# Splitting the last output tile of a fused attention and feed-forward kernel, with an older start order

## The chip, the cores and the metric

One NeuronCore of a Trainium2 chip. The metric is the device time of one execution in microseconds, as a median over runs; a profiled execution beside it says where the time goes. The engines that matter: TensorE (PE, with its weight loads shown apart as PEld), VectorE (DVE), ScalarE (ACT), GpSimd (POOL), and SyncE (SP), which issues most transfers. Each runs its own list of instructions in order and waits on semaphores.

## The reference

Linear attention for 8 batches, 8 heads, 576 positions and head size 64, then a feed-forward layer with a swish that has one beta for each of its 2048 units:

```python
q_s = softmax(q, over the head's 64 numbers)
k_s = softmax(k, over the 576 positions)
kv  = einsum('bhsd,bhse->bhde', k_s, v)
x   = einsum('bhsd,bhde->bhse', q_s, kv)      # to 4608 x 512
h   = x @ w_in                                # 4608 x 2048
g   = h * sigmoid(beta * h)
out = g @ w_out                               # 4608 x 512, float32
```

Inputs and output are float32; inside, the kernel multiplies in bfloat16 and sums in float32.

## The kernel before

The 4608 tokens go through in nine slabs of 512: slab t < 8 holds the first 512 positions of batch t, and slab 8 the last 64 positions of all eight batches. For each slab there is a first product (16 units f of 128 hidden columns, each 4 matmuls over the input pairs m, into a PSUM bank, then ACT's Silu into `GT`) and a second product (four token tiles u of 128, each 16 matmuls over f with 512 output columns, then a copy to `O2S` and a store). "Input pair" m is a pair of heads, 128 of the 512 inputs. Attention work for the next batch is woven into these matmuls by tick counts: `todo` holds (tick, step), and `tick()` runs what is due.

Everything is in the program order of one Python list; `Program` derives the waits from keys read and written and sends each instruction to its engine's list. So a line's place in the program sets its place in its engine's order, transfers on SP's and ACT's lists too.

The start, batch 0 and batch 1, is written out by hand:

- Loads on SP: q and k of batch 0, v of batch 0 (`load_v`, four transfers), then W_in in blocks (`load_win(c, m)`: c is a group of 512 hidden columns, that is 4 units; m the input pair), then W_out (`load_wout`), with batch 1's q, k, v between. W_in and W_out land as float32 in stage buffers; `cast_win` casts W_in blocks to bf16 on POOL or DVE, and `scale_wout` multiplies W_out tile f by 1/beta on DVE (L555).
- Batch 0: exponentials on ACT, the normalising of q on DVE and POOL, transposes of q on PE (`t_steps`, with a copy `QT<-PS`, L384), K-V products (`kv_mm`), `ksum_inv` and `kvd` (KVD is the K-V product divided by the sums, L518 and L403), the output product `out_now` with its copy `XT<-PS` (L530).
- `by_m` runs four units of the first product at once, input pair by input pair, so that a weight block is used as soon as it is cast; `pass1_tile` runs one unit over all its four pairs. `FIRST` says how many units go by `by_m`: 16 of slab 0 and 5 of slab 1.
- In slab 0's second product all four token tiles go side by side, f outermost, so that each W_out tile is used when it has been scaled. At ticks 107 and 112 the transposes of batch 1's q come in, at 115 and 117 the K-V products of its first two head pairs, at 122 and 123 `out_now` for them.

W_in's and W_out's hidden columns are ordered so that a row of a weight transfer is contiguous: units 0 to 7 are interleaved in pairs (`f // n * n`, `f % n` with n = 2), units 8 to 15 in fours.

From the second batch on the transposes are done by the transfer engines, and the attention steps are spread over the slabs' ticks.

Slab 8's output tile u is copied by DVE (L713) when its 16 matmuls are done and stored by `store8` in two transfers of 64 rows, one issued by SP and one by ACT.

Of the kernel before, what the change touches and what calls it, by code (L numbers as in the profile page):

```python
# [156 lines left out]
def bass_efficient_attn_shen__then__act_swish_beta_kernel(  # L157
# [12 lines left out]
    with ExitStack() as es:  # L170
# [367 lines left out]

        STAGE = (WST[0], WST[1], O2S[1], O2S[0])
# [3 lines left out]
        def load_wout(f, n=4):  # L543
            c, x = f // 4, f % 4
            if f < 8:
                a = bass.AP(wout_h, 512 * c * DM, [[2 * DM, 128], [256 * DM, 2], [1, 2 * DM]])
                o = bass.AP(STAGE[c], 0, [[4 * DM, 128], [2 * DM, 2], [1, 2 * DM]])
            else:
                a = bass.AP(wout_h, (512 * c + x) * DM, [[4 * DM, 128], [1, n * DM]])
                o = bass.AP(STAGE[c], x * DM, [[4 * DM, 128], [1, n * DM]])  # L550
            add(SP, lambda e: e.dma_start(o, a), w=SKEY[c][x:x + n], slot=f"wst{f}")  # L551
# [19 lines left out]
        def turn_beta():  # L571
            for g, n, o in ((4, 4, 0), (2, 2, 0), (2, 2, 256)):
                for k_ in range(n):
                    mm(bass.AP(PS[KB], 16 + o // 128 + k_, [[512, 128], [4, g]]),
                       bass.AP(BT, o + k_, [[512, g], [n, 128]]), IDF[0:g, 0:g],
                       True, True, r=["bt", "idf"], w=[("ps", KB)], bk=KB, tr=True)
# [33 lines left out]
        load_v(0, 4, (0, 1, 2))  # L610
        load_win(0, 0, 1)
        load_v(0, 4, (3,))
        for c in range(4):
            for m in range(0 if c else 1, NM, 1 if c < 2 else 2):
                load_win(c, m, 1 if c < 2 else 2)
# [3 lines left out]
        cast_win(0, 0, POOL)  # L619
        cast_v(0, 3)  # L620
        cast_win(0, 2, POOL)
        cast_win(0, 3, POOL)
        cast_win(1, 0, POOL)
# [9 lines left out]
        kvd(0, 1, 1, 0)  # L633

        orot = [0]

        def pass1_mm(t, f, m, bk):
            x = XT8 if t == 8 else XT[t % 2]
            rd = [("xt8", p_) for p_ in range(4)] if t == 8 else [("xt", t % 2, m)]
            n = 2 if f < 8 else 4  # L640
            l = bass.AP(WIN, m * DFF + 128 * (f // n * n) + f % n, [[NM * DFF, 128], [n, 128]])
# [24 lines left out]
        FIRST = (16, 5)  # L666
# [4 lines left out]
        cast_win(0, 1, DVE)  # L671
        out_now(0, 1, 6, ACTE)
        at = by_m(0, 0, 4)
        at(0, 0, 3)
        kv_mm(0, 3, 1, 0, D + 1)
        at(0, 3)
        out_now(0, 2, 0, ACTE)
        ksum_inv(0, 1, 3, 1, D, 1)
        kvd(0, 3, 1, 0)
        at(1)  # L680
        out_now(0, 3, 7, DVE)
# [5 lines left out]
        for c in range(1, 4):  # L687
            for m in range(1 if c == 1 else 0, NM):
# [3 lines left out]
        for g in (4, 8, 12):  # L692
# [3 lines left out]
        for e_ in range(2):  # L696
            homes_ek(1, e_, [("win", 3, NM - 1)])
# [24 lines left out]
        def store8(u):  # L722
# [174 lines left out]
```

## Time and profile before

| what | value |
|---|---|
| median of 4 runs | 286.53 us (286.35 to 286.71) |
| the profiled execution's own time | 286.16 us |
| its span, first to last instruction | 284.4 us |
| PE busy | 275.3 us, 97% of the span |
| ACT / DVE / POOL busy | 177.9 / 117.2 / 39.5 us |
| matmuls of 512 columns, first product / second product | 131.4 us / 131.4 us |
| first matmul with weights of W_in | 13.51 us |
| first matmul of the second product | 28.61 us |
| first output product of batch 1 | 43.41 us |
| last copy of an output tile | 280.55 us, 0.69 us long |
| granted TensorE clock | 1.0 |

Times in the lists are microseconds from the span's start. A line of the timeline gives start, duration, engine, source line, operation, tiles written and read, shapes, how many such instructions are merged, and in brackets how long the engine was idle before and which instruction ended that. Group lines give busy time in us and the mean of one instruction in ns.

### The profile page before, as it was taken

Reading aid. Unit: us, or ns where it says so; the run is one execution under the profiler, and the core shown is the slowest. Engines: PE = TensorE matmul, PEld = TensorE weight load, DVE = VectorE, ACT = ScalarE, POOL = GpSimd, SP = SyncE. Lnnn points to the kernel's source line nnn. Section 1 sums busy time; section 2 is a strip of 40 time slices with the busy share of each in tenths; the row PEclk is TensorE's granted clock in tenths of the full one; section 3 lists DMA queues with packets and bytes.
Section 4 is the critical chain, followed back from the end, with each engine's and each line's share of the span. In section 5 each row is a group of like instructions: output and inputs, shape, how many; then the busy total and the mean of one; then the engine's idle time right before and its main releaser. Section 6 shows DMA issues by size and latency. Waiting matters only on the chain.

```text
span 284.4 us, 3851 instructions
## 1 busy us (share of the span) xinstructions
PE 275.3 (97%) x1543; PEld 135.1 (48%) x1573; DVE 117.2 (41%) x216; ACT 177.9 (63%) x242; POOL 39.5 (14%) x59
## 2 busy tenths in 40 slices
PE   6899999999999999999999999999999999999994
PEld 2545454445455445544554445444544444444441
DVE  4863896019881348123831473045705200110021
ACT  5967777989978926795579637892650185028400
POOL 6622041307122033100230000000000000000000
PEclk9999999999999999999999999999999999999999
DMA  7999999996998999217970033003500120021022
GB/s 245 349 393 400 388 386 377 352 385 121 312 362 228 369 362 298 39 38 262 364 95 1 2 149 72 2 1 129 111 2 0 45 105 0 0 92 58 0 74 74
DMA packets 41306, 50.07 MB, mean 176 GB/s; under 512 B 20292, under 2 KB 28484, under 8 KB 40136
## 3 DMA queue, kind: packets, MB, share of 16 engines
q1 hardware_dynamic: 40416, 48.77, 53.5%
q10 hardware_dynamic: 872, 1.06, 1.0%
q8 instruction: 12, 0.20, 0.3%
q14 instruction: 6, 0.05, 0.1%
HBM read 36.71 MB, written 9.44 MB: 162 GB/s over the span
## 4 chain that ended last, share of the span: by engine, by line
PE 83%; DMA 7%; SPq 5%; ACT 2%; issue 1%; DVE 1%; ACTq 0%
PE PS L366 83%; DMA O2S<-in_moe_w_in_dram 4%; DMA KF<-in_k_dram 3%; SPq L259 2%; SPq L249 2%; SPq L562 1%; ACT EK L317 1%; ACT QT L384 0%; DVE WIN L566 0%; DVE O2S L713 0%; ACT GT L645 0%; ACT XT L530 0%; ACT O2S L713 0%; SPq L551 0%; ACTq L140 0%
## 5 line engine op out<-in xcount | busy, mean ns | idle before, releaser
L645 ACT ACTIVATE GT<-PS,BETA 128x512 bf16<-128x512 f32 x144 | 96.5, 688 | 79.2 <-PE PS L366 79.1
L366 PE MATMUL PS<-WOUT,GT 128*128 128x512 bf16 x563 | 131.4, 379 | 1.3 <-ACT QT L384 0.6
L366 PE MATMUL PS<-XT,WIN 128*128 128x512 bf16 x561 | 131.4, 379 | 0.6
L366 PEld LDWEIGHTS PS<-XT,WIN 128*128 128x128 bf16 x576 | 60.1, 106 | 59.5 <-POOL WIN L566 0.9
L366 PEld LDWEIGHTS PS<-WOUT,GT 128*128 128x128 bf16 x576 | 54.2, 98 | 63.5 <-DVE WOUT L555 0.9
L713 DVE COPY O2S<-PS 128x512 f32<-128x512 f32 x34 | 23.4, 687 | 110.5 <-PE PS L366 110.5
L366 PE MATMUL PS<-VB,EK 128*128 128x65 bf16 (+2 forms) x306 | 35.8, 191 | 1.1 <-ACT VB L351 0.6
L351 POOL CAST VB<-VF 128x576 bf16<-128x576 f32 x31 | 23.1, 747 | 73.8 <-DMA VF<-in_v_dram 36.2
L307 ACT ACTIVATE EK<-KF 64x1152 bf16<-64x1152 f32 x24 | 27.8, 1157 | 0.4
L366 PEld LDWEIGHTS PS<-VB,EK 128*128 128x128 bf16 x306 | 22.0, 98 | 7.7 <-ACT VB L351 0.5
L332 DVE TENSOR_REDUCE QS<-EQ 128x8 f32<-128x512 bf16 (+1 forms) x22 | 20.1, 914 | 3.7 <-ACT EQ L295 3.5
L441 DVE CAST XT<-PS 128x512 bf16<-128x512 f32 x24 | 16.4, 690 | 10.9 <-PE PS L366 10.9
L295 ACT ACTIVATE EQ<-QF 128x512 bf16<-128x512 f32 x32 | 17.8, 618 | 2.7 <-DMA QF<-in_q_dram 2.5
L334 DVE TENSOR_TENSOR EQ<-EQ,QI 128x1024 bf16<-128x1024 bf16 (+1 forms) x15 | 16.5, 1103 | 0.5
L366 PE MATMUL PS<-QT,KVD 128*128 128x512 bf16 x30 | 11.4, 379 | 0.0
L317 ACT ACTIVATE EK<-KF 64x576 bf16<-64x576 f32 (+1 forms) x12 | 9.9, 839 | 1.9 <-DMA KF<-in_k_dram 1.8
L334 POOL TENSOR_TENSOR EQ<-EQ,QI 128x512 bf16<-128x512 bf16 x7 | 7.4, 1051 | 19.8 <-DVE QI L333 19.5
L403 DVE TENSOR_TENSOR KVD<-PS,RC 64x64 bf16<-64x64 f32 (+2 forms) x28 | 8.6, 308 | 1.1 <-PE PS L364 0.2
L340 DVE TENSOR_REDUCE QRS<-EQR 128x8 f32<-128x512 bf16 x4 | 2.7, 681 | 13.1 <-ACT EQR L322 13.1
L366 PE MATMUL PS<-XT 128*128 128x512 f32 x10 | 6.6, 793 | 1.5 <-DVE XT L219 1.5
L295 ACT ACT_TABLE_LOAD x5 | 6.4, 1283 | 0.1
L645 ACT ACT_TABLE_LOAD x5 | 6.4, 1283 | 0.1
(51 smaller groups left out, 77.1 us busy)
## 6 DMA issues: line engine op xcount, KB each, us to landing
out_dram<-O2S SPq DMA_DIRECT2D x8, 1024.0 KB, 5.1
KF<-in_k_dram SPq DMA_DIRECT2D x6, 1152.0 KB, 8.2
VF<-in_v_dram SPq DMA_DIRECT2D x6, 1152.0 KB, 11.2
QF<-in_q_dram SPq DMA_DIRECT2D x6, 1024.0 KB, 7.6
KF<-in_k_dram SPq DMA_DIRECT2D x8, 288.0 KB, 7.9
VF<-in_v_dram SPq DMA_DIRECT2D x8, 288.0 KB, 8.9
WST<-in_moe_w_in_dram SPq DMA_DIRECT2D x8, 256.0 KB, 8.2
O2S<-in_moe_w_in_dram SPq DMA_DIRECT2D x4, 512.0 KB, 11.7
```

The lines of the kernel that those rows point to most:

```text
L249: add(engs[c % len(engs)], lambda e, c=c: e.dma_start(dst(bufs[i], c * n, n), src(th, b, c * n, n)), w=[(name, i, hp) for hp in range(c * ...
L295: add(ACTE, lambda e, o=o, a=a: e.activation(o, a, ACT.Exp), r=[("qf", i, hp)], w=[("eq", i, hp)])
L307: add(ACTE, lambda e, o=o, a=a: e.activation(o, a, ACT.Exp), r=[("kf", i, h) for h in hps], w=[("ek", i, h, e_) for h in hps])
L317: add(ACTE, lambda e: e.activation(o, a, ACT.Exp), r=[("kf", i, h) for h in hps], w=[("ek", i, h, e_) for h in hps])
L332: add(DVE, lambda e: e.tensor_reduce(s_, a, AX.X, ALU.add), r=ks, w=[("qs", i, hp0)])
L334: add(eng, lambda e: e.tensor_tensor(a, a, vb, ALU.mult), r=ks + [("qi", i, hp0)], w=ks)
L351: add(eng, lambda e: (e.copy if eng == ACTE else e.tensor_copy)(o, a), r=[("vf", i, hp), ("vone", i)], w=[("vb", i, hp, h) for h in ((0, 1 ...
L366: add(PE, lambda e: e.matmul(o, l, r_, start=start, stop=stop), r=r, w=w, bank=[bk])
L403: add(DVE, lambda e, o=o, a=a, s_=s_: e.tensor_tensor(o, a, s_, ALU.mult), r=[("ps", bk)] + [("rc", i, h) for h in hps], w=[("kvd", i, h, ...
L441: add(eng, lambda e: (e.copy if eng == ACTE else e.tensor_copy)(XT[i][:, hp, :], PS[bk][:, :]), r=[("ps", bk)], w=[("xt", i, hp)], bank=[bk])
L645: add(ACTE, lambda e: e.activation(GT[:, f, :], PS[bk][:, :], ACT.Silu, scale=BETA[:, f:f + 1]), r=[("ps", bk), "beta"], w=[("gt", f)], ba ...
L713: add(eng, lambda e: (e.copy if eng == ACTE else e.tensor_copy)(O2S[t % 2][:, u, :], PS[bk][:, :]), r=[("ps", bk)], w=[("o2", t % 2, u)], ...
```

## The change

Ten edits in one diff, of which the first concerns the end and the others the start:

1. The last output tile (slab 8, u = 3) is made in two parts: 16 matmuls for its columns 0 to 383 into one bank, then 16 for columns 384 to 511 into another, each part copied by DVE and stored by two transfers of its own.
2. All units are interleaved in fours: in the slice of W_in that a unit takes, in W_out's transfers for units 0 to 7 (rows of 8 KB instead of two of 4 KB), and in the transposes of beta (4 instead of 8).
3. All four value transfers of batch 0 stand before the first W_in block on SP's list; before, the first W_in block stood between the third and the fourth.
4. The W_in block (0, 0) is cast by DVE, placed after KVD of pair 1, instead of by POOL; block (0, 1) by POOL instead of DVE; block (1, 0) by DVE instead of POOL.
5. In slab 0's first four units, the K-V product of pair 3 and its KVD come before the first of these matmuls, which then go four, two, two, and on by pairs.
6. The copy of batch 0's output 2 goes from ACT to DVE, that of output 3 from DVE to ACT.
7. `FIRST[0]` goes from 16 to 12: units 12 to 15 of slab 0 go one after another by `pass1_tile`.
8. POOL's zeroing of batch 1's EK waits for the last W_in block of group 2 instead of group 3.
9. The copies of batch 1's transposed q go from ACT to DVE.
10. ACT's exponentials of batch 1's k, head pair 2, move from tick 112 to before slab 0's second product.

```diff
+        load_v(0, 4)
...
         def load_wout(f, n=4):
             c, x = f // 4, f % 4
-            if f < 8:
-                a = bass.AP(wout_h, 512 * c * DM, [[2 * DM, 128], [256 * DM, 2], [1, 2 * DM]])
-                o = bass.AP(STAGE[c], 0, [[4 * DM, 128], [2 * DM, 2], [1, 2 * DM]])
-            else:
-                a = bass.AP(wout_h, (512 * c + x) * DM, [[4 * DM, 128], [1, n * DM]])
-                o = bass.AP(STAGE[c], x * DM, [[4 * DM, 128], [1, n * DM]])
+            a = bass.AP(wout_h, (512 * c + x) * DM, [[4 * DM, 128], [1, n * DM]])
+            o = bass.AP(STAGE[c], x * DM, [[4 * DM, 128], [1, n * DM]])
...
         def turn_beta():
-            for g, n, o in ((4, 4, 0), (2, 2, 0), (2, 2, 256)):
-                for k_ in range(n):
-                    mm(bass.AP(PS[KB], 16 + o // 128 + k_, [[512, 128], [4, g]]),
-                       bass.AP(BT, o + k_, [[512, g], [n, 128]]), IDF[0:g, 0:g],
-                       True, True, r=["bt", "idf"], w=[("ps", KB)], bk=KB, tr=True)
+            for k_ in range(4):
+                mm(bass.AP(PS[KB], 16 + k_, [[512, 128], [4, 4]]),
+                   bass.AP(BT, k_, [[512, 4], [4, 128]]), IDF[0:4, 0:4],
+                   True, True, r=["bt", "idf"], w=[("ps", KB)], bk=KB, tr=True)
...
-        load_v(0, 4, (0, 1, 2))
-        load_win(0, 0, 1)
-        load_v(0, 4, (3,))
         for c in range(4):
-            for m in range(0 if c else 1, NM, 1 if c < 2 else 2):
+            for m in range(0, NM, 1 if c < 2 else 2):
                 load_win(c, m, 1 if c < 2 else 2)
         cast_v(0, 0)
         cast_v(0, 1)
         cast_v(0, 2, ACTE)
-        cast_win(0, 0, POOL)
         cast_v(0, 3)
-        cast_win(0, 2, POOL)
-        cast_win(0, 3, POOL)
-        cast_win(1, 0, POOL)
+        for m in range(1, NM):
+            cast_win(0, m, POOL)
...
         kv_mm(0, 1, 1, 0)
         kvd(0, 1, 1, 0)
+        cast_win(0, 0, DVE)
...
-            n = 2 if f < 8 else 4
-            l = bass.AP(WIN, m * DFF + 128 * (f // n * n) + f % n, [[NM * DFF, 128], [n, 128]])
+            l = bass.AP(WIN, m * DFF + 512 * (f // 4) + f % 4, [[NM * DFF, 128], [4, 128]])
...
-        FIRST = (16, 5)
+        FIRST = (12, 5)
         out_now(0, 0, 0, ACTE)
         kv_mm(0, 2, 7, 0, D + 1)
         ksum_inv(0, 7, 2, 1, D, 1)
         kvd(0, 2, 7, 0)
-        cast_win(0, 1, DVE)
         out_now(0, 1, 6, ACTE)
-        at = by_m(0, 0, 4)
-        at(0, 0, 3)
         kv_mm(0, 3, 1, 0, D + 1)
-        at(0, 3)
-        out_now(0, 2, 0, ACTE)
         ksum_inv(0, 1, 3, 1, D, 1)
         kvd(0, 3, 1, 0)
-        at(1)
-        out_now(0, 3, 7, DVE)
+        at = by_m(0, 0, 4)
+        at(0)
+        out_now(0, 2, 0, DVE)
+        at(1, 0, 2)
+        out_now(0, 3, 7, ACTE)
+        at(1, 2)
...
         for c in range(1, 4):
-            for m in range(1 if c == 1 else 0, NM):
+            for m in range(NM):
                 cast_win(c, m, DVE)
...
-        for g in (4, 8, 12):
+        for g in (4, 8):
...
-            homes_ek(1, e_, [("win", 3, NM - 1)])
+            homes_ek(1, e_, [("win", 2, NM - 1)])
...
-        def store8(u):
+        def store8(u, c0=0, c1=DM, key=None):
             for h in range(2):
-                a = bass.AP(out_h, ((2 * u + h) * S + SM) * DM, [[DM, 64], [1, DM]])
+                a = bass.AP(out_h, ((2 * u + h) * S + SM) * DM + c0, [[DM, 64], [1, c1 - c0]])
                 add(SP if h == 0 else ACTE,
-                    lambda e, h=h, a=a: e.dma_start(a, O2S[0][64 * h:64 * h + 64, u, :]),
-                    r=[("o2", 0, u)], slot=f"outr{u}{h}")
+                    lambda e, h=h, a=a: e.dma_start(a, O2S[0][64 * h:64 * h + 64, u, c0:c1]),
+                    r=[key or ("o2", 0, u)], slot=f"outr{u}{h}{c0}")
+
+        def last_tile(u, parts, bks):
+            for (c0, c1), bk in zip(parts, bks):
+                for f in range(NF):
+                    mm(PS[bk][:, 0:c1 - c0], GT[:, f, 128 * u:128 * u + 128], WOUT[:, f, c0:c1],
+                       f == 0, f == NF - 1, r=[("gt", f), ("wout", f)], w=[("ps", bk)], bk=bk)
+                add(DVE, lambda e, c0=c0, c1=c1, bk=bk: e.tensor_copy(
+                    O2S[0][:, u, c0:c1], PS[bk][:, 0:c1 - c0]),
+                    r=[("ps", bk), ("o2", 0, u)], w=[("o2c", c0)], bank=[bk])
+                store8(u, c0, c1, ("o2c", c0))
...
-                todo = [(107, lambda: go(t_steps(1, (0, 1), (1,), ACTE))),
-                        (112, lambda: go(t_steps(1, (2, 3), (2,), ACTE))),
-                        (112.1, lambda: (scale_wout(14, 2), exp_kh(1, 2, 1, 0), exp_kh(1, 2, 1, 1))),
+                todo = [(107, lambda: go(t_steps(1, (0, 1), (1,)))),
+                        (112, lambda: go(t_steps(1, (2, 3), (2,)))),
+                        (112.1, lambda: scale_wout(14, 2)),
...
                 exp_kh(1, 0, 2, 0)
                 exp_kh(1, 0, 2, 1)
+                exp_kh(1, 2, 1, 0)
+                exp_kh(1, 2, 1, 1)
...
             for u in range(4):
+                if (t, u) == (8, 3):
+                    last_tile(u, ((0, 384), (384, 512)), (OB[orot[0] % 2], MB[0]))
+                    continue
                 pass2_group(t, (u,), (OB[orot[0] % 2],), tick)
```

## The prediction

> **What bounds the kernel now.** I read the page first, its totals and its chain of work that ended last.
>
> ```profile
> PE 275.3 (97%) x1543; PEld 135.1 (48%) x1573; DVE 117.2 (41%) x216; ACT 177.9 (63%) x242; POOL 39.5 (14%) x59
> ...
> PE 83%; DMA 7%; SPq 5%; ACT 2%; issue 1%; DVE 1%; ACTq 0%
> ```
>
> TensorE (PE) is busy for 97% of the span and carries 83% of the chain. From 46.7 us on the chain is PE alone, so time lost or won before that point reaches the end in full, and only two places can move: the start (to about 44 us) and the tail after the last matmul. The start runs on a transfer queue served in order: by the trace's landings (the last of a transfer's 16 counts) the value block of head pair 2 is there at 11.57 us, the first W_in block at 12.79, value pair 3 at 13.55, the other first-group blocks at 14.20, 14.88 and 15.56, the last two W_in transfers at 23.76 and 25.11, W_out's first two groups at 27.66 and 30.29, and its last two tiles at 40.58 and 41.26. Nothing in the diff removes bytes, so these stand.
>
> Next the timelines of VectorE (DVE), GpSimd (POOL) and PE around 35 to 44 us.
>
> ```profile
> 37.89 0.64 DVE L332 TENSOR_REDUCE QS<-EQ 128x8 f32<-128x512 bf16 x1
> 38.56 0.20 DVE L333 RECIPROCAL QI<-QS 128x8 f32<-128x8 f32 x1
> 38.80 0.91 DVE L334 TENSOR_TENSOR EQ<-EQ,QI 128x512 bf16<-128x512 bf16 x1
> 39.63 2.47 DVE L555 TENSOR_SCALAR WOUT<-O2S,RB 128x512 bf16<-128x512 f32 x4
> 42.45 0.17 DVE L518 RECIPROCAL RC<-PS 128x2 f32<-128x2 f32 x1 [0.35 <-PE PS L366]
> 42.66 0.61 DVE L403 TENSOR_TENSOR KVD<-PS,RC 64x128 bf16<-64x128 f32 x2
> ```
> ```profile
> 39.30 1.74 POOL L351 CAST VB<-VF 128x576 bf16<-128x576 f32 x2
> 42.75 0.67 POOL L351 CAST VB<-VF 128x576 bf16<-128x576 f32 x1 [1.71 <-DMA VF<-in_v_dram]
> ```
> ```profile
> 42.23 1.24 PE L366 MATMUL PS<-WOUT,GT 128*128 128x512 bf16 x5
> 43.41 0.38 PE L366 MATMUL PS<-QT,KVD 128*128 128x512 bf16 x1
> ```
>
> DVE has no idle time from 32.33 us (the reduction after batch 1's first q exponential) until 42.10; it then waits 0.35 us for PE's K-V product, makes KVD, and PE's first output of batch 1 follows at 43.41. That 0.35 us is all the slack DVE has. The four scalings of W_out (L555) also show a coupling: alone one takes 0.47 us, but beside a POOL instruction it ends 0.28 us after POOL does. Tiles 12 and 13 end at 40.51 and 41.32, where POOL's two casts end at 40.23 and 41.04; tiles 0 and 9 do the same. The KVD products, which read PSUM, ran beside POOL's cast at 42.75 at their usual 0.28 to 0.30 us.
>
> Last the tail, and the copies' row of the groups.
>
> ```profile
> 278.84 1.67 PE L366 MATMUL PS<-WOUT,GT 128*128 128x512 bf16 x7
> ...
> 280.55 0.69 DVE L713 COPY O2S<-PS 128x512 f32<-128x512 f32 x1 [2.76 <-PE PS L366]
> 281.27 0.47 SPq L726 DMA_DIRECT2D out_dram<-O2S  x1
> 281.27 0.50 ACTq L726 DMA_DIRECT2D out_dram<-O2S  x1
> ```
> ```profile
> L384 DVE COPY QT<-PS 128x512 bf16<-128x512 bf16 x4 | 1.6, 408 | 0.3 <-PE PS L366 0.3
> ```
>
> After the last matmul: 0.69 us of copy, two stores that land 2.32 and 2.62 us after issue (283.59 and 283.89), and 0.5 us to the end.
>
> **First weight block: near nothing.** Value pair 3 now goes ahead of the first W_in block on SP's queue: pair 3 should land near 12.4 to 12.8, the block at 13.55. Its cast moves to DVE, which waits there from about 12.7; behind it in DVE's order stand the sums and KVD of pairs 2 and 3 and the copy of output 2 that leaves ACT for DVE. From the rows: cast 0.43 (13.60 to 14.03), 0.17 + 0.47 twice with 0.03 gaps (to 15.45), copy 0.69 (to 16.17). PE needs that copy at 16.2 for the third input pair, so its second group starts near 17.95, against 18.03 before. The four beta transposes that go (0.12 us each) lie before 12.66, where PE waits for a value cast. In 18 to 29 us a slip up to 0.3 either way meets the landings.
>
> **Fourth group unit by unit: 0.15 us, then covered.** PE reaches it at 24.85. By pairs it wants the third block at 26.6; unit by unit at 25.3, while the casts end at 25.56 and 25.89. That stalls about 0.48 us, so the second product starts at 28.76 instead of 28.61 (where it had waited for W_out's first tile; that tile is earlier now, since POOL's zeroing of EK leaves 26.02 for about 21.8). PE then waits for DVE near 40 us anyway. In exchange Silu ends near 29.65 instead of 30.36, ACT's first q exponentials start 0.7 earlier (q lands at 30.90), and DVE can start the dense stretch when W_out tile 7 is scaled, at 31.92 instead of 32.33: 0.41 us gained on that chain.
>
> **Transposed q copied by DVE: +0.5 us.** Two copies of 128x1024 bf16 leave ACT (1.01 us each there, in time it spends waiting for K, which lands at 42.02 regardless; so the two K exponentials moved ahead win nothing) and go to DVE between W_out tiles 13 and 14. The trace has no such copy on DVE. From 512 to 1024 columns it lies between once and twice the 0.42 us row; f32 at 512 takes 0.69 where bf16 takes 0.42, so a fixed part near 0.15 and 0.27 per 512 give 0.69. I take 0.69, ends 0.42 and 0.85. Chain: tile 13 ends at 40.95 (bound by POOL's cast, 41.32 before), copies to 41.56 and 42.17, tiles 14 and 15 to 42.95, reciprocal and KVD 0.8 to 43.78, PE at 43.9. Before: 43.41. PE has been ready since about 42.95, and behind that product wait the other outputs of batch 1 and all of the second slab; so +0.5 us, with ends +0.1 and +0.85.
>
> **Weights and loads: nothing.** Units in fours instead of pairs make the load of eight units' weights stride 8 bytes instead of 4: the groups in two windows of slab 8, units 0 to 7 and then 8 to 15, price that.
>
> ```profile
> L366 PEld LDWEIGHTS PS<-XT,WIN 128*128 128x128 bf16 x32 | 3.1, 97 | 3.8
> ...
> L366 PEld LDWEIGHTS PS<-XT,WIN 128*128 128x128 bf16 x32 | 3.6, 113 | 3.3
> ```
>
> 16 ns more, hidden under matmuls 215.8 ns apart in both windows. W_out's first two groups come in rows of 8 KB instead of 4; a 1 MB group took 2.55 to 2.63 us in one form and 2.57 in the other.
>
> **Tail: -0.42 us.** The last sixteen 512-column matmuls (215.5 ns apart) become sixteen of 384 and sixteen of 128. At 384 I scale to 162 ns: 2.60 us. For 128 columns the trace has the transposes, each with its own weights, eight in a row at 55 ns starts (37.93 to 38.32): 0.89. Sum 3.49 against 3.45, so the last matmul ends 0.04 later. The first copy (about 0.55) and its two stores run beside the 128-column matmuls and are done by 280.8. The last copy has 128 f32 columns; KVD reads 128 such in 0.29 us, so 0.40 less. Its stores carry a quarter of the bytes: their first counts came 2.06 and 2.38 us after issue and the last 2.32 and 2.62, so between 0 and 0.25 less; I take 0.06, near the unchanged end, since two more stores are under way. Sum -0.42, ends -0.2 and -0.6.
>
> The Trainium skill speaks against this part: TensorE: Matmul & The Clock Gate, Back-to-back issue gap, gives about 81 ns for sustained 128-column pairs of weight load and matmul; the 55 ns of this trace's transposes contradict it, and by the page's figure the tail would win about 0.4 less, that is nothing. DMA: Bandwidth & Descriptors, Rules for kernel authors, advises joining small transfers because under 64 KB one pays mostly overhead; here the overhead is what the 2.06 us first counts show, and it is paid in parallel with the matmuls for the first pair of stores.
>
> **Sum.** Profiled execution: 286.16 us, span 284.4 with 1.76 around it, 0.37 under the median 286.53. +0.5 and -0.42 give +0.08: 286.24 in such an execution, 286.6 as a median. Less than 0.2% (0.57 us, about what a measurement of this kernel can tell from no change).
>
> **The rivals.**
> *Slower, by the POOL coupling (0.28).* POOL's cast of value pair 2 starts at 42.75 whatever else happens (it lands at 42.70). I have W_out tile 15 start at 42.48. If the chain is 0.27 us later, as with copies of 0.85, the scaling waits to 43.42 + 0.28 = 43.70, KVD ends at 44.5, PE goes at 44.65: +1.24 instead of +0.5, net +0.8, 287.3 us. For it: the four scalings that POOL held. Against: the margin is there by the rows.
> *Faster, by the same coupling (0.16).* Tile 12's scaling now starts at 39.22, where POOL's cast of pair 0 starts too (landing 39.14). If DVE is first, the chain wins about 0.4 to 0.7; PE's own work allows the product from 42.95. Start about -0.2, net -0.6: 285.9 us.
> *The split does not pay (0.06).* If the weight loads of the 128-column matmuls (98 ns each by their row of W_out, GT) don't overlap the matmuls as the transposes' did, sixteen take 1.57 us instead of 0.89: tail +0.26, net +0.8, 287.3 us.
> *My forecast (0.50):* 286.6, own range 286.1 to 287.1.
>
> Faster 0.16; same 0.50; slower 0.28 + 0.06 = 0.34. The range 286.0 to 287.4 leaves out about half of the faster case and a third of the slower ones.
>
> **What would show it.** In the changed profile: two DVE copies of 128x1024 between W_out scalings, near 0.69 us; PE idle near 43 us before the first QT,KVD product at about 43.9, released by DVE's KVD; a short PE stall near 25.5 us; second product from 28.8. In the tail: 128-column starts 55 ns apart, a last copy near 0.29 us, last landing about 2.5 us after its issue. It is wrong if W_out tile 15 ends past 43.5 or before 42.5, if PE's second group starts after 18.5, or if PE idles elsewhere after 50 us.

## The result, and the profile after

| | before | after |
|---|---|---|
| median | 286.52 us (56 runs, 285.99 to 287.38) | 285.89 us (34 runs, 284.86 to 287.01) |
| ratio of the medians | | 0.9974, 95% interval 0.9968 to 0.9981 |
| profiled execution, its span | 286.16, 284.4 us | 285.39, 283.6 us |

The change is faster by 0.26%, below the range of the prediction. The runs of the changed kernel lie in two groups of 17: 284.86 to 285.74 and 286.04 to 287.01. The profiled execution is of the lower one, so the profile below explains −0.77 us; the upper group has its own section.

The page of the changed kernel, its totals and its chain:

```profile
PE 275.9 (97%) x1555; PEld 138.7 (49%) x1585; DVE 119.5 (42%) x220; ACT 176.0 (62%) x240; POOL 39.0 (14%) x58
...
PE 82%; DMA 7%; DVE 5%; SPq 3%; ACT 1%; issue 1%
```

PE is busy about as long as before (275.9 us, 275.3 before) and still carries most of the chain; DVE's share of the chain has grown from 1% to 5%: that is the start, whose timeline on DVE follows (start, duration, engine, line; in brackets the idle time before and what ended it).

```profile
29.62 1.67 DVE L553 TENSOR_SCALAR WOUT<-WST,RB 128x512 bf16<-128x512 f32 x4 [0.98 <-DMA WST<-in_moe_w_out_dram]
31.22 0.69 DVE L332 TENSOR_REDUCE QS<-EQ 128x8 f32<-128x512 bf16 x1
...
38.52 1.75 DVE L553 TENSOR_SCALAR WOUT<-O2S,RB 128x512 bf16<-128x512 f32 x2
40.19 1.27 DVE L384 COPY QT<-PS 128x1024 bf16<-128x1024 bf16 x2
41.39 0.86 DVE L553 TENSOR_SCALAR WOUT<-O2S,RB 128x512 bf16<-128x512 f32 x2
42.17 0.15 DVE L518 RECIPROCAL RC<-PS 128x2 f32<-128x2 f32 x1
42.37 0.61 DVE L403 TENSOR_TENSOR KVD<-PS,RC 64x128 bf16<-64x128 f32 x2
```

Before, the stretch began like this, waiting for ACT's exponentials after the last of the scalings:

```profile
30.31 1.67 DVE L555 TENSOR_SCALAR WOUT<-WST,RB 128x512 bf16<-128x512 f32 x4 [0.67 <-DMA WST<-in_moe_w_out_dram]
32.33 0.69 DVE L332 TENSOR_REDUCE QS<-EQ 128x8 f32<-128x512 bf16 x1 [0.35 <-ACT EQ L295]
```

PE and POOL at the same place:

```profile
41.26 1.26 PE L366 MATMUL PS<-WOUT,GT 128*128 128x512 bf16 x5
43.03 0.39 PE L366 MATMUL PS<-QT,KVD 128*128 128x512 bf16 x1 [0.51 <-DVE KVD L403]
```
```profile
42.12 0.67 POOL L351 CAST VB<-VF 128x576 bf16<-128x576 f32 x1 [2.13 <-DMA VF<-in_v_dram]
```

The two new copies stand between the scalings and take 0.67 us each; PE waits 0.51 us for KVD. From the end of W_out tile 13 to the output product it now takes 2.76 us (40.27 to 43.03), where it took 2.09 (41.32 to 43.41). But DVE's dense stretch starts at 31.22 instead of 32.33, so the first output product of batch 1 comes at 43.03 us, where it was 43.41: the start wins 0.38 us although it has more work.

The tail: the matmuls of the last tile by form, in the groups of the stretch from 278.4 us, then the two copies, then the issues of the last stores (engine, count, KB, median us from issue to landing).

```profile
L366 PE MATMUL PS<-WOUT,GT 128*128 128x384 bf16 x9 | 1.6, 326 | 0.0
L366 PE MATMUL PS<-WOUT,GT 128*128 128x128 bf16 x16 | 1.1, 219 | 0.0
```
```profile
279.74 0.56 DVE L725 COPY O2S<-PS 128x384 f32<-128x384 f32 x1 [1.91 <-PE PS L366]
280.64 0.29 DVE L725 COPY O2S<-PS 128x128 f32<-128x128 f32 x1 [0.34 <-PE PS L366]
```
```profile
out_dram<-O2S SPq DMA_DIRECT2D x1, 32.0 KB, 2.0
out_dram<-O2S ACTq DMA_DIRECT2D x1, 32.0 KB, 2.2
```

The sixteen 128-column matmuls take 1.1 us in all. The last store lands at 283.12 us, 2.16 us after its issue at 280.96; before, it landed at 283.89, 2.62 us after 281.27.

What lies between start and tail is seen by setting the starts of PE's weight loads side by side:

| first weight load of | before | after | difference |
|---|---|---|---|
| slab 1, first product | 45.21 | 44.84 | −0.37 |
| slab 2, unit 8 | 84.17 | 83.87 | −0.29 |
| slab 3, unit 8 | 114.01 | 113.79 | −0.22 |
| slab 5, unit 8 | 173.47 | 173.42 | −0.05 |
| slab 6, unit 8 | 203.08 | 203.13 | +0.05 |
| slab 8, second product | 266.32 | 266.37 | +0.05 |

So the profiled −0.77 is a start of −0.37, a loss of 0.42 in slabs 2 to 6, and a tail of −0.82.

### The profile page after: what moved, and what is told of

Its sections match the earlier page's. It is cut to its first block, busy times and chain, and to the rows that moved or that the text cites. A ratio compares the mean times of both kernels' runs of the same rounds, so it can differ in the third digit from the quotient of the medians.

```text
span 283.6 us, 3876 instructions
## 1 busy us (share of the span) xinstructions
PE 275.9 (97%) x1555; PEld 138.7 (49%) x1585; DVE 119.5 (42%) x220; ACT 176.0 (62%) x240; POOL 39.0 (14%) x58
## 4 chain that ended last, share of the span: by engine, by line
PE 82%; DMA 7%; DVE 5%; SPq 3%; ACT 1%; issue 1%
PE PS L366 82%; DMA WST<-in_moe_w_out_dram 4%; DMA WST<-in_moe_w_in_dram 3%; DVE WOUT L553 2%; SPq L259 1%; SPq L560 1%; DVE QS L332 1%; DVE EQ L334 1%; ACT EK L317 0%; DVE QT L384 0%; SPq L249 0%; DVE QI L333 0%; ACT GT L637 0%; DVE KVD L403 0%; ACT XT L530 0%
## 5 line engine op out<-in xcount | busy, mean ns | idle before, releaser
L366 PE MATMUL PS<-WOUT,GT 128*128 128x512 bf16 (+2 forms) x579 | 131.4, 373 | 0.6
L366 PEld LDWEIGHTS PS<-XT,WIN 128*128 128x128 bf16 x576 | 64.5, 113 | 57.1 <-issue 0.7
L366 PEld LDWEIGHTS PS<-WOUT,GT 128*128 128x128 bf16 x592 | 55.2, 98 | 62.1 <-DVE WOUT L553 0.3
L704 DVE COPY O2S<-PS 128x512 f32<-128x512 f32 x33 | 22.7, 687 | 107.7 <-PE PS L366 107.7
L366 PEld LDWEIGHTS PS<-VB,EK 128*128 128x128 bf16 x306 | 22.6, 99 | 8.1 <-POOL VB L351 0.9
L332 DVE TENSOR_REDUCE QS<-EQ 128x8 f32<-128x512 bf16 (+1 forms) x22 | 20.1, 914 | 3.1 <-ACT EQ L295 3.0
L441 DVE CAST XT<-PS 128x512 bf16<-128x512 f32 x24 | 16.4, 690 | 10.9 <-PE PS L366 10.9
L366 PE MATMUL PS<-XT 128*128 128x512 f32 x10 | 7.2, 853 | 1.5 <-DVE XT L219 1.5
```

Of the source, the lines that this page charges most:

```text
L332: add(DVE, lambda e: e.tensor_reduce(s_, a, AX.X, ALU.add), r=ks, w=[("qs", i, hp0)])
L366: add(PE, lambda e: e.matmul(o, l, r_, start=start, stop=stop), r=r, w=w, bank=[bk])
L441: add(eng, lambda e: (e.copy if eng == ACTE else e.tensor_copy)(XT[i][:, hp, :], PS[bk][:, :]), r=[("ps", bk)], w=[("xt", i, hp)], bank=[bk])
L704: add(eng, lambda e: (e.copy if eng == ACTE else e.tensor_copy)(O2S[t % 2][:, u, :], PS[bk][:, :]), r=[("ps", bk)], w=[("o2", t % 2, u)], ...
```

## Experiments: the tail, and the loss in slabs 2 to 6

**The split alone** (kernel before, edit 1 only).

```diff
...
+                if (t, u) == (8, 3):
+                    last_tile(u, ((0, 384), (384, 512)), (OB[orot[0] % 2], MB[0]))
+                    continue
...
```

> The kernel before with nothing but the last output tile split in 384 and 128 columns. Theory A (the tail gives more than forecast, since the last stores land 2.16 us after issue instead of 2.62): about -0.8 us against the kernel before, slabs 0 to 7 unchanged. Theory B (the forecast's terms: copy -0.40, matmuls +0.04, stores -0.06): -0.42 us. Theory C (weight loads of 98 ns not overlapped): +0.26 us.

Median 285.72 (6 runs, 285.49 to 286.06), ratio 0.9973 (0.9961 to 0.9985); profiled execution 285.49, span 283.7. Its last tile starts 0.13 us later than before's, so its tail wins 0.83 of a span 0.7 shorter. Its last stores:

```profile
out_dram<-O2S SPq DMA_DIRECT2D x1, 32.0 KB, 2.0
out_dram<-O2S ACTq DMA_DIRECT2D x1, 32.0 KB, 2.1
```

The last issue is at 281.04, the last landing at 283.19, 2.15 us later. The split alone is worth about 0.8 us; the forecast's 0.42 falls. About half of it is the copy (0.69 to 0.29 us), the other half the landing (2.62 to 2.15 us after issue).

**The start alone** (the changed kernel with the last tile whole).

> The changed kernel with its last output tile whole again, so the start's edits alone. Theory A (start about -0.4 us because transfers land 0.5 to 0.7 us earlier, and slabs 2 to 6 lose 0.42 us together): within 0.1 us of the kernel before. Theory B (the forecast: two copies on VectorE cost 0.5 us, nothing lost later): +0.5 us. Theory C (the start's gain in the profiled execution was chance, the later loss is real): +0.4 to +0.9 us.

Median 286.27 (12 runs, 285.67 to 287.88), ratio 0.9993 (0.998 to 1.0007). By the weight loads: −0.27 in slab 1, +0.42 through slabs 2 to 6, and the last landing again 2.62 us after issue (281.42 to 284.04). Nine edits of the ten come to nothing that can be measured: two effects that cancel, not none.

**Units in fours alone** (kernel before, edit 2 only).

```diff
-            n = 2 if f < 8 else 4
-            l = bass.AP(WIN, m * DFF + 128 * (f // n * n) + f % n, [[NM * DFF, 128], [n, 128]])
+            l = bass.AP(WIN, m * DFF + 512 * (f // 4) + f % 4, [[NM * DFF, 128], [4, 128]])
...
```

> The kernel before with one change: all units interleaved in fours (W_in's slices, W_out's transfers, beta's transposes). Theory A (weight loads of 113 ns instead of 97 are not hidden where 65-column matmuls stand between the 512-column ones): 0.05 to 0.08 us lost in each of slabs 2 to 6, in their first eight units and nowhere else, +0.4 us in all. Theory B (the forecast: hidden): 0.0 us, and the later loss of the changed kernel has another cause.

Median 287.03 (11 runs, all but one far outlier from 286.71 to 287.30), ratio 1.0008 (0.9989 to 1.0027). The medians alone can't tell; the profile can. Its start was 0.68 us late, as the first W_in block and value pair 3 landed 0.68 and 0.65 later than in before's profile; why isn't known, and the stages after the start are compared by their lengths. Units 0 to 7 of slabs 2 to 6 take 8.24 and four times 8.12 us, where before's take 8.16 and four times 8.04; slabs 1, 7 and 8 take the same in both (7.73, 6.91, 6.91). That is 0.40 us, in those units and in no other of these slabs. The weight loads in slab 3's first eight units (106.1 to 113.8 us), in the kernel before and then in the changed one, where the two numbers behind the first bar are busy us and mean ns:

```profile
L366 PEld LDWEIGHTS PS<-XT,WIN 128*128 128x128 bf16 x31 | 3.0, 98 | 3.0
L366 PEld LDWEIGHTS PS<-VB,EK 128*128 128x128 bf16 x31 | 2.8, 97 | 0.8
```
```profile
L366 PEld LDWEIGHTS PS<-XT,WIN 128*128 128x128 bf16 x31 | 3.5, 113 | 2.9
L366 PEld LDWEIGHTS PS<-VB,EK 128*128 128x128 bf16 x31 | 2.9, 100 | 0.8
```

The 512-column matmuls follow each other 215.8 ns apart, with loads of 98 and of 113 alike: the longer load is covered. In these units the K-V products' 65-column matmuls stand between, which are far shorter than a load. Where one stands between two matmuls of the first product, the two weight loads of the latter start 256.4 ns apart in the kernel before and 259.8 in this run and in the changed kernel; the 95 such places that can be counted in slabs 2 to 6 sum to 0.32 of the 0.40 us. Slab 8 has none, and there the longer load costs nothing. That the short matmuls are what exposes it is read from the place; no run moved them.

## Experiments: the start

**Value pair 3 ahead of the first W_in block, alone** (kernel before, edit 3 only).

```diff
         load_v(0, 4, (0, 1, 2))
-        load_win(0, 0, 1)
         load_v(0, 4, (3,))
+        load_win(0, 0, 1)
```

> The kernel before with one change: value pair 3 is issued ahead of the first W_in block. Theory A (the first reads of W_in come late by about 0.5 us, and a value transfer ahead of them hides that): value pair 3 lands near 12.4 us, the first W_in block near 13.1, everything behind it 0.4 to 0.5 earlier, W_out's first group near 27.2; first output of batch 1 0.2 to 0.4 us earlier than 43.41; -0.2 to -0.4 us. Theory B (the order is worth nothing, the 0.7 us in the changed kernel's profile came from elsewhere or by chance): first W_in block at 13.5, W_out at 27.6, 0.0 us.

Median 286.84 (11 runs), ratio 1.0003 (0.9994 to 1.0012). The stream does come earlier: the first W_in block and value pair 3 are both in at 13.01 us, 13.55 before, and W_out's groups land at 27.01 and 29.62, 0.65 earlier. But DVE waits 1.23 us for ACT, 0.35 before:

```profile
32.55 0.69 DVE L332 TENSOR_REDUCE QS<-EQ 128x8 f32<-128x512 bf16 x1 [1.23 <-ACT EQ L295]
```
```profile
30.59 1.28 ACT L295 ACT_TABLE_LOAD   x1
31.89 1.15 ACT L295 ACTIVATE EQ<-QF 128x512 bf16<-128x512 f32 x2
```

ACT's Silu of the fourth group ends at 30.57 (30.36 before), and only then come the exponentials. The landings moved as the first theory said; the time did not.

Where the stream's time comes from is seen in the transfers from 9 to 16 us, before and then after (GB/s in 40 slices of 0.175 us, and the sum):

```profile
GB/s 408 408 421 421 408 356 420 401 382 322 307 247 176 105 94 97 146 218 271 379 392 395 429 378 421 410 375 410 433 386 410 410 398 398 421 398 398 410 398 398
DMA packets 1294, 2.46 MB, mean 351 GB/s; under 512 B 144, under 2 KB 144, under 8 KB 1294
```
```profile
GB/s 421 395 408 408 421 408 421 395 395 408 408 394 417 400 364 277 199 257 176 269 410 386 398 398 433 398 421 386 398 398 410 386 421 339 281 316 339 351 410 386
DMA packets 1374, 2.61 MB, mean 373 GB/s; under 512 B 154, under 2 KB 154, under 8 KB 1374
```

Before, the rate falls to 94 GB/s near 11.5 us, where the first W_in block is read: 29 of its 128 packets take 200 ns or more, up to 625, where about 85 is usual. After, 10 do, up to 289, and the dip goes to 176 only. The 0.15 MB more in the stretch are 0.38 us at 400 GB/s, without a byte removed.

A transfer counts as landed with the last of its 16 counts, and the last one varies: in every trace one or a few of the 16 fall behind on the way, so that W_out's first group lands 1.4 to 2.1 us after its middle count (the median of the 16). The middle counts tell the order apart: W_out's first group has it at 25.79 to 25.94 us in the four traces with the block first, and at 25.41 to 25.57 in the fourteen with value pair 3 first. So of the 0.71 us by which this group lands earlier in the changed kernel (26.95, 27.66 before), 0.42 goes with the order (25.50 and 25.92 by the middle counts); the rest is the straggling count, and the traces show no order in it.

**The control of what follows.** All kernels from here on leave out one thing: for batches 2 to 7 and the remainders the transfer engines copy q instead of transposing it, the same bytes, from 64 us on. So their output is not the reference's from slab 2 on, and what follows is shown for these kernels and carried over to the changed one, on which the same edits were not run. The control is otherwise the changed kernel.

> The control of this group: the changed kernel with the transposes of q for batches 2 to 7 and of the remainders, done by the transfer engines from 64 us on, replaced by plain copies of the same size. Its output is not the reference's from slab 2 on; nothing before 60 us is touched. All theories: start as in the changed kernel (first output of batch 1 near 43.0 us), time within 0.3 us of it.

Control: median 285.38 (12 runs: 7 at 284.87 to 285.42, 5 at 286.12 to 286.87), ratio 0.9963 (0.9949 to 0.9977); profiled execution 285.09, first output product of batch 1 at 42.76. So it stands for the changed kernel in the start, with the two groups too (medians of the lower ones 285.26 and 285.30). One thing differs in the profiles: the scaling of W_out tiles 12 and 13.

```profile
38.72 1.27 DVE L554 TENSOR_SCALAR WOUT<-O2S,RB 128x512 bf16<-128x512 f32 x2
```

It starts 0.11 us ahead of POOL's cast (38.83) and takes 1.27 us; in the changed kernel's profile both start at 38.52, POOL holds DVE, and it takes 1.75. The control a second time, beside other kernels and on another chip:

> The control once more, beside the kernels of this group. All theories: two groups of runs, near 285.2 and 286.3. If the profiled execution is of the upper group, theory A expects W_out's tile 14 or 15 to be scaled 0.28 us past the end of POOL's cast near 42.5 us, and the first output of batch 1 near 44 us; theory B expects the first output near 43 us and the loss elsewhere.

Median 285.11 (5 runs, 284.88 to 285.33), ratio 0.9948 (0.9936 to 0.9961): that time only the lower group.

**The first block put back ahead** (control, edit 3 undone).

> The control with the first W_in block again between the third and the fourth value transfer. Theory A (the first reads of W_in come late and the fourth value transfer hides that): W_in's first block and value pair 3 together take 2.0 to 2.4 us behind value pair 2 instead of 1.4, W_out's tiles 4 to 7 land near 30.2 instead of 29.6, VectorE's chain starts near 31.9 instead of 31.2; 0.4 to 0.8 us over the control. Theory B (the order is not the cause): landings and time as in the control.

Median 286.56 (11 runs, 285.89 to 286.88), ratio 0.9985 (0.9976 to 0.9994): 1.2 us above the control, more than either theory gave. That is not the order alone: edit 5 has put the K-V product of pair 3 ahead of the first matmuls with W_in, and value pair 3 now lands at 13.87 (12.17 in the control), so PE waits 1.17 us for its cast and these matmuls start at 14.95 instead of 13.84. From the landing of value pair 2 until block and value pair 3 are both in took 2.27 us (control 1.81, before 1.98), DVE's stretch starts at 32.06 instead of 31.30, after a wait for ACT's exponentials, and then a second thing comes on top:

```profile
42.16 1.35 DVE L552 TENSOR_SCALAR WOUT<-O2S,RB 128x512 bf16<-128x512 f32 x2
43.43 0.15 DVE L519 RECIPROCAL RC<-PS 128x2 f32<-128x2 f32 x1
```

Tiles 14 and 15 take 1.35 us, 0.86 in the changed kernel: tile 15 ends 0.28 us after POOL's cast (42.56 to 43.23).

**The fourth group by pairs again** (control, edit 7 undone).

```diff
-        FIRST = (12, 5)
+        FIRST = (16, 5)
...
-        for g in (4, 8):
+        for g in (4, 8, 12):
```

> The control with units 12 to 15 of slab 0 by input pair again. Theory A (the early landings pay only if ACT is free: unit by unit, Silu ends 0.8 to 1.1 us earlier, and the first q exponentials of batch 1 let VectorE's chain start at 31.2): Silu ends near 30.1, chain starts near 32.0, first output of batch 1 near 43.8; 0.6 to 0.9 us over the control. Theory B (the forecast: 0.41 us on the chain): 0.4 us. Theory C (the transfers alone set the start): 0.0 us or a little less, as the stall of 0.3 to 0.5 us at unit 12 goes.

Median 286.64 (11 runs, 286.50 to 286.96), ratio 0.9994 (0.9986 to 1.0003), 1.3 us above the control, more than any theory gave. W_out is there at 29.66, yet:

```profile
32.21 0.69 DVE L332 TENSOR_REDUCE QS<-EQ 128x8 f32<-128x512 bf16 x1 [0.86 <-ACT EQ L295]
...
42.32 1.25 DVE L554 TENSOR_SCALAR WOUT<-O2S,RB 128x512 bf16<-128x512 f32 x2
```

Silu ends at 30.24 (29.06 in the control), and tile 14 is held by POOL. In this execution POOL's zeroing of EK (22.90 to 25.23) also held group 3's casts, which end at 26.18 instead of 25.28, so the later Silu is not edit 7's alone.

**Both edits, put into the kernel before** (edits 3 and 7, nothing else of the change).

> The kernel before (with plain copies in place of the transfer engines' transposes) with two edits of the change: value pair 3 ahead of the first W_in block, and units 12 to 15 of slab 0 one after another; its copies of transposed q stay on ACT, its last tile stays whole. Theory A (each alone gives nothing, together they let VectorE's chain start near 31.3 instead of 32.3 us): first output of batch 1 near 42.7 instead of 43.4 us, -0.5 to -0.8 us against the kernel before. Theory B (the gain needs the moved casts and the other order of the first four units as well): within 0.2 us of the kernel before.

Median 285.69 (7 runs, 285.56 to 285.93), ratio 0.9972 (0.9961 to 0.9983). DVE's stretch starts at 31.80, the first output product of batch 1 comes at 43.02, and the profile is ahead of before's by 0.39 from there to the end (285.77 to 286.16); the medians differ by more, 0.97, mostly since the profiled execution of before lies 0.50 under its median here. The first theory's 42.7 and 31.3 were not reached. The start of DVE's stretch shows the pair best: 32.33 before, 32.55 with edit 3 alone, 32.21 where the control lacks edit 7, 32.06 where it lacks edit 3, 31.80 with both and 31.30 in the control. So the pair gives 0.53 of the control's 1.03 us, and edit 3 alone gives nothing. The rest comes from other edits of the start: here unit 4 of slab 0 starts at 18.58, in the control at 17.73, and Silu ends at 29.82 instead of 29.06. The new order of casts and first matmuls (edits 4 to 6) lies at this place; no run took these edits apart.

**The copies of transposed q back to ACT** (control, edits 9 and 10 undone).

```diff
-                todo = [(107, lambda: go(t_steps(1, (0, 1), (1,)))),
-                        (112, lambda: go(t_steps(1, (2, 3), (2,)))),
-                        (112.1, lambda: scale_wout(14, 2)),
+                todo = [(107, lambda: go(t_steps(1, (0, 1), (1,), ACTE))),
+                        (112, lambda: go(t_steps(1, (2, 3), (2,), ACTE))),
+                        (112.1, lambda: (scale_wout(14, 2), exp_kh(1, 2, 1, 0), exp_kh(1, 2, 1, 1))),
...
-                exp_kh(1, 2, 1, 0)
-                exp_kh(1, 2, 1, 1)
```

> The control with the copies of batch 1's transposed q back on ACT, and ACT's exponentials of k, head pair 2, back behind them. Theory A (the forecast's term is right: these copies cost VectorE's chain about 0.5 us, and the start gained in spite of them): first output of batch 1 near 42.4 us, 0.5 to 0.6 us under the control. Theory B (the copies are hidden, the forecast erred in this term): within 0.1 us of the control.

Median 284.98 (5 runs, 284.73 to 285.45), ratio 0.9935 (0.9922 to 0.9948), 0.40 under the control and 0.28 under its lower group. On DVE the scalings run through and the wait for PE is back:

```profile
38.45 2.52 DVE L554 TENSOR_SCALAR WOUT<-O2S,RB 128x512 bf16<-128x512 f32 x4
41.32 0.17 DVE L519 RECIPROCAL RC<-PS 128x2 f32<-128x2 f32 x1 [0.35 <-PE PS L366]
41.53 0.61 DVE L403 TENSOR_TENSOR KVD<-PS,RC 64x128 bf16<-64x128 f32 x2
```

The output product comes at 42.28, 0.48 earlier than in the control's first profile; the control's two other profiles of the lower group have it at 42.52 and 42.41. Executions differ in when the stretch starts and in whether POOL holds tiles 12 and 13 (it does here). From the end of tile 13 to the output product they agree: 2.12 us here, 2.76 or 2.77 with the copies on DVE where tiles 14 and 15 are not held. So the copies cost about 0.65 us on this chain. In this execution 0.47 us were lost again in slab 1's second product; the control repeated lost 0.18 there, and the cause isn't known.

## Experiments: the two groups of runs

The prediction's slower rival was that W_out tile 15 meets POOL's cast and waits for its end. In the changed kernel's profile, which is of the lower group, it does not: tile 15 starts at 41.78, the cast at 42.12. Two edits were tried, each taking away one place where POOL holds DVE.

**Value pair 2 of batch 1 cast by ACT** (control with):

```diff
-                    cast_v(1, hp)
+                    cast_v(1, hp, ACTE if hp == 2 else POOL)
```

> The control (the changed kernel with plain copies in place of the transfer engines' transposes) with one cast moved: batch 1's value pair 2 is cast by ACT instead of POOL, so that no POOL instruction lies beside VectorE's scaling of W_out tiles 14 and 15. The runs of the changed kernel and of the control fall into two groups about 1 us apart. Theory A (the upper group is the coupling: in those executions POOL's cast starts before the scaling of tile 15 and holds it to 0.28 us after its own end): the upper group is gone, all runs within 0.4 us of the lower group, near 285.2. Theory B (the groups come from the transfers or the stores): two groups as before, at 285.2 and 286.3.

Median 285.79 (12 runs: ten at 285.06 to 285.89, then 286.19 and 286.72), ratio 0.9969 (0.9959 to 0.9979). Tiles 14 and 15 took 0.87, unheld, yet DVE's stretch had started at 31.74: W_in's casts of group 3 had been held by POOL's zeroing of EK (22.70 to 25.04). Two runs of twelve are still above 286, and the other ten reach up to 285.89, where the control's lower group ends at 285.42; beside this kernel, on the same chip, the control had none above 286 in five. So moving the cast is not enough; the zeroing is a second coupling.

**Zeroing of EK back to after group 3** (control, edit 8 undone).

```diff
-            homes_ek(1, e_, [("win", 2, NM - 1)])
+            homes_ek(1, e_, [("win", 3, NM - 1)])
```

> The control (plain copies in place of the transfer engines' transposes) with one edit undone: POOL's zeroing of batch 1's EK waits again for the last W_in block of group 3. Theory A (the early zeroing lies beside VectorE's casts of group 3 and holds them to 0.28 us after POOL; in executions where the casts end late, Silu ends late, VectorE's chain starts late, and the scaling of W_out tile 15 is caught by POOL's cast at 42.5 us): casts of group 3 take 0.43 us each, fewer runs in the upper group near 286.3. Theory B (the zeroing is harmless): share of the upper group as in the control, 5 of 17 or more.

Median 285.17 (6 runs: five at 284.88 to 285.43, one 286.38), ratio 0.995 (0.9934 to 0.9967). The zeroing now stands behind the last two casts:

```profile
24.59 0.76 DVE L565 CAST WIN<-O2S 128x512 bf16<-128x512 f32 x2 [0.59 <-DMA O2S<-in_moe_w_in_dram]
```
```profile
25.48 2.17 POOL L236 MEMSET EK<- 64x1152 f32 x2 [9.20 <-DVE WIN L565]
```

In this execution W_in's third group landed late, at 21.88 (20.62 in the control's first profile). Yet the casts of group 3 take 0.42 each, DVE's stretch starts at 31.19, and the time is 284.91: a late landing without the zeroing beside the casts cost nothing. One run of 6 in the upper group, against 5 of 12, proves nothing by count.

**Both edits.**

> The control with both POOL couplings taken away: the zeroing as late as in the kernel before, and batch 1's value pair 2 cast by ACT. Theory A: one group of runs, 284.9 to 285.6, and none at 286 or more. Theory B: two groups as in the control.

Median 285.30 (6 runs, 284.75 to 285.95), ratio 0.9945 (0.9932 to 0.9958). No run reaches 286, where the control has 5 of 12 on one chip and 0 of 5 on another. But the profiled execution, 285.95, had W_in's third group at 22.36 and W_out's second at 30.20, and DVE's stretch at 31.82: late landings alone shift the stretch, without POOL. And a third coupling was left in: tiles 12 and 13 (39.11 to 40.89) were held by POOL's casts of pairs 0 and 1.

**Two more single executions of the control**, to catch the upper group.

> The control once more, for a profile. Theory A: if its time is over 286.0, W_out's tile 14 or 15 is scaled 0.28 us past the end of POOL's cast near 42.5 us and the first output of batch 1 comes near 44 us; under 285.6, the first output comes near 43 us. Theory B: no such link.

> As the look before it: a time over 286.0 goes with a scaling held by POOL's cast and a first output of batch 1 near 44 us (theory A), or with a loss elsewhere (theory B).

The first was of the lower group (284.75, span 283.0), the second of the upper (286.30, span 284.5). DVE, POOL and PE of the second:

```profile
23.19 2.84 DVE L565 CAST WIN<-O2S 128x512 bf16<-128x512 f32 x4 [0.56 <-DMA O2S<-in_moe_w_in_dram]
...
31.79 0.69 DVE L332 TENSOR_REDUCE QS<-EQ 128x8 f32<-128x512 bf16 x1 [0.55 <-ACT EQ L295]
...
41.89 1.28 DVE L554 TENSOR_SCALAR WOUT<-O2S,RB 128x512 bf16<-128x512 f32 x2
```
```profile
22.75 2.33 POOL L236 MEMSET EK<- 64x1152 f32 x2 [5.65 <-DVE WIN L565]
...
42.19 0.70 POOL L351 CAST VB<-VF 128x576 bf16<-128x576 f32 x1 [1.69 <-DMA VF<-in_v_dram]
```
```profile
43.94 0.39 PE L366 MATMUL PS<-QT,KVD 128*128 128x512 bf16 x1 [0.87 <-DVE KVD L403]
```

W_in's third group landed at 21.84 (20.62 in the control's first profile), so POOL's zeroing started 1.2 us later and lay across the casts of group 3, which took 2.84 us and ended at 26.03 (25.28 there). Silu ended at 29.81, DVE's stretch started at 31.79, tile 15 ran into POOL's cast (42.19 to 42.89) and ended 0.28 us after it. Against the profile of the changed kernel the stretch starts 0.57 later, of which 0.50 is left at tile 14, and the held tile adds 0.42; together that is the 0.91 by which the output product is later. So in the execution caught, the upper group is the rival's mechanism, set off by a late landing; with the zeroing out of the way the same late landing did no harm. That every run of the group is like this, and how often it comes, stays open: removing both couplings left no such run in 6, removing one left 1 in 6 and 2 in 12, but these were on other chips than the control's 5 in 12, and the control itself had 0 in 5 on another occasion.

## A version with units in pairs and the copies on ACT

Control with units in pairs as before (edit 2 undone) and the copies on ACT (edits 9 and 10 undone):

> The control with units 0 to 7 interleaved in pairs again and the copies of batch 1's transposed q on ACT: the changed kernel's good parts without its two bad ones. Theory A (pairs are worth 0.42 us in slabs 2 to 6 less 0.15 us for rows of 4 KB in W_out's first two groups; the copies 0.4 to 0.6 us): 284.5 to 284.8, one group of runs. Theory B (neither adds to the copies on ACT alone): 285.0.

Median 284.92 (6 runs, 284.51 to 285.72), ratio 0.9947 (0.9934 to 0.996); profiled execution 284.51, span 282.7, the shortest seen. Units 0 to 7 of slabs 3 to 6 take 8.04 us again, so by slab 7 it is 0.65 ahead of the control's profile. The weight loads of slab 3's first units are back:

```profile
L366 PEld LDWEIGHTS PS<-XT,WIN 128*128 128x128 bf16 x30 | 3.0, 100 | 2.7
```

By the ratio it is 1.5 us under before, with the transposes replaced as said; with them it wasn't run. Its median is not clearly lower than that of the copies on ACT alone (284.98), nor than the control's beside it on the same chip (285.11, ratio 0.9948). Against that control's profile it wins 0.48 by slab 7: 0.32 in slabs 3 to 6, by the pairs, and the rest in slab 1's second product, where that control lost 0.18. At the start nothing shows of the copies: the output products come at the same time (42.55 and 42.52), as the stretch starts 0.24 later here and POOL holds tiles 12 and 13 (1.68 us, 1.27 there). So the gain of the pairs shows in the profile; that this version beats the control in the median is not shown.

## Why the prediction was wrong

The profiled execution was forecast at 286.24 and took 285.39. The 0.85 between are three terms: −0.87 at the start, +0.42 in the weights, −0.40 in the tail.

- **"Nothing in the diff removes bytes, so these stand" failed.** The sum took W_out's landings at 27.66 and 30.29; they came at 26.95 and 29.60. Moving one transfer past another hid part of the slow first reads, which is worth about 0.4 us by the middle counts; the rest of the 0.7 is the straggling count, which varies between executions, so that part is luck. The forecast had the fourth group's gain (edit 7) limited by exactly that landing: DVE's stretch starts at 31.22, not 31.92.
- **"First weight block: near nothing" failed too.** PE's second group was forecast at 17.95, against 18.03 before, since the block was kept at its landing of 13.55; it landed at 13.07, and the group started at 17.56. Edits 3 and 7 alone, without the new order of casts and first matmuls, reached a stretch start of 31.80 only. So of the 1.11 us by which the stretch starts earlier, the forecast had 0.41; landings, unit order and the first units' order together gave it, and edit 3 alone, in the kernel before, gave none of it.
- **The copies on VectorE were over-priced.** The +0.5 of the sum already contained the 0.41 that the stretch was to start earlier: by its own rows the forecast has 2.95 us from the end of tile 13 (40.95) to the output product (43.9), where 2.09 were before, so 0.86 for the copies. They cost 0.67 (2.76). Their duration (0.67, forecast 0.69) and PE's wait for KVD were right. With the earlier stretch (0.68 at tile 13) this makes the output product 0.87 earlier than forecast.
- **"Weights and loads: nothing" failed by 0.42.** The 113 against 97 ns were read rightly, and as covered by matmuls 215.8 ns apart, but in slab 8, the one place priced, no short matmul stands between. The trace of before held slabs 2 to 6 as well.
- **The tail was mis-sized: −0.82 for −0.42.** Copies (0.56 and 0.29) and matmul spacing were as worked out: the 384-column ones start 162.5 ns apart, the 128-column ones 55.8. The stores' landing was given 0.06; it was 0.46, outside the stated bounds of 0 to 0.25. Those took it that fewer bytes shorten the spread from first to last count. The spread stayed (0.25 and 0.23 us); the first counts came 1.74 and 1.93 us after issue, where they had come after 2.06 and 2.38.
- **The stall** forecast near 25.5 us came before the fourth group instead, 0.34 us by the weight loads: its first cast, 23.13 to 24.47, was held by POOL's zeroing (22.02 to 24.19), an edit that the forecast counted as a gain only.
- **The rivals.** The slower one named the right mechanism and a margin of 0.27 us (0.34 in the changed kernel's profile); the one execution of the upper group that was caught shows it, set off by a late landing rather than slow copies, at about 1 us. It didn't make the change slower, since tail and start had won more by then. The faster one, DVE ahead of POOL at tile 12, did not happen in the changed kernel's profile, where both start at 38.52; in the four profiles of lower-group speed of the control and of its late-zeroing version it did, by 0.05 to 0.11 us. That the change came out faster is thus not this rival's doing in the execution that was profiled. That the split wouldn't pay is refuted: the sixteen 128-column matmuls start 55.8 ns apart, not 98. The Trainium skill's 81 ns for sustained 128-column pairs (TensorE: Matmul & The Clock Gate, Back-to-back issue gap) does not agree with these sixteen pairs with weights of their own.

## What to carry to other kernels

A landing time in a trace is a result of the queue's order, not a given: ask of every moved transfer what it would cover or uncover. Where several waits end within half a microsecond, price their removal together, since one alone can buy nothing. And price a slower instruction at every place where it runs, above all where its cover is shortest.

## What the runs showed of the hardware

- The first reads of W_in were partly slow: 29 of the first block's 128 packets took 200 to 625 ns against about 85. With the block first the next two landings took 1.98 to 2.36 us in four executions, with the value block first 1.38 to 1.94 in fourteen.
- The first count of a store of 64 rows, issued by SP, came 2.06 us after issue with 2 KB a row, 1.89 with 1.5 KB and 1.74 with 512 bytes. Why isn't known.
- A DVE scaling or cast from fp32 in SBUF ended 0.28 us after the POOL instruction that it met, POOL's zeroing included (24.47 after 24.19); the KVD products, which read PSUM, were not held. The Trainium skill (SBUF — State Buffer, Who interferes with whom) has a port pair that one of the two holds for a whole instruction, and the held scalings agree.
- One transfer of 16 KB of instructions took 1.04 to 1.13 us in each trace, starting between 17.2 and 21.5 us. In the kernel before (20.82 to 21.87) one of the 16 counts fell behind the others at this place (22.30 and 23.76 us for the last two of the W_in transfer that landed next), and all later landings on that queue stayed late. That the one caused the other is read from the times, not tested. The caught execution lagged by 1.9 us between first and last count from 16.4 us on, before its own transfer of instructions at 20.1, and has another, unknown cause. The Trainium skill (Runtime: NRT & Kernel Launch, Instruction fetch mechanics) calls the cost of crossing a 16 KiB boundary mostly hidden; here DVE's scalings waited 0.98 us on a landing behind it (29.60).
